# Running two first-stage units of an FFT back to back on TensorE, correction term first

## The chip, the core and the metric

The kernel runs on one core of a Trainium2 chip. The metric is the device time of one execution in microseconds (us); smaller is better. A core has a matrix engine (PE, whose weight loads the profile lists apart as PEld), a vector engine (DVE), a scalar engine (ACT), a general engine (POOL) and SP, which in this kernel only issues DMAs. Each engine takes its instructions in the order in which they stand in its own queue, and waits on semaphores for the others.

## The reference

Eight sequences of 2496 tokens with 256 channels go through a filter in the frequency domain and then through a soft mixture of experts (8 experts, 32 slots in all). All is float32.

```python
X = np.fft.rfft(x, axis=1)
y = np.fft.irfft(X * (filt_r + 1j * filt_i)[None], n=x.shape[1], axis=1)
x = y.reshape(B * S, D)
logits = x @ phi
d = softmax of logits over the tokens;  slot_input = d.T @ x
slot_out[e] = relu(slot_input[e] @ w1[e]) @ w2[e]
c = softmax of logits over the slots;   out = c @ slot_out
```

## The kernel before, in words

The transform over 2496 = 39 x 64 tokens is done in two stages of matrix products. A batch is one sequence.

**First stage** (`split_x`, `s1_unit`). The 64 columns of a batch are taken six at a time, in 11 units u per batch, b being the batch. The transform matrix and the data are each split into a high part that TensorE's float32r form holds exactly and a low part, the remainder: `w1h`, `w1l` for the matrix, `xh`, `xl` for the data. `xh` is a cast on ACT (L317), `xl` a subtraction on POOL that needs the cast (L318). The unit is then three products into one PSUM tile (L328): `w1h` with `xh`, `w1l` with `xh`, and `w1h` with `xl`, which is ready last. ACT copies the tile to `at` (L329), and SP issues a DMA of that to DRAM (`a_dram`, L333 to L336). `xh` and `xl` have three buffers each, the PSUM pool `ps_s1` two banks, `at` five buffers. One input tile `xt` (three buffers) holds the data of two units, an even one and the odd one behind it. Batch 0 takes another way into stage two (L285, L299), without the split.

**Second stage** (`x_unit`, `t_unit`). Ten steps c per batch. `ash` is read back from `a_dram` by a DMA (L349). `x_unit` multiplies it by a 128x128 matrix (L359; four matmuls in the program, eight in the trace), DVE multiplies the result by the filter's two parts (L372, L373), and the two halves are added, one on DVE (L375), one on POOL (L376, the tile `yt`). From batch 6 on, POOL does both. `t_unit` transposes `yt` on TensorE (L384), ACT copies it out to `y` (L386); at the end of a batch 40 small products make its logits (L399, `l`, 80 in the trace).

**The chain.** After every second batch a chain of further products (`chain`, L424 on) forms the maximum, the exponentials `d` and the slot sums from the two batches: `ltr`, `v`, `lg`, `mt`, `mb`, `u`, `dd`, `s`. Its steps are dealt out two at a time between the slots described next. Those of the last pair of batches run after the loop, and then come the experts and the output.

**What sets the order.** A loop over slots n, ten to a batch, puts in program order: the loads of `ash` five slots ahead, the split (`split_next`) of the units of slot n+1, then `x_unit` of n, the first-stage units whose slot is n, `t_unit` of n-2, and two steps of the chain. The slot of unit u of batch b (L679) is ten slots per batch plus min(u, 9), less five; so from batch 2 on one unit comes in each slot and units 9 and 10 share one. Batch 1's eleven units share the first five slots. After the split of an odd unit the next `xt` load is issued. A list scheduler then makes each engine's queue out of that program order, by priorities of its own; so the order on an engine has to be read from the built program. In names like `s_3_5` of that order, 3 is the batch and 5 the unit; `t_6` of the same place is `t_unit` of step 6; the last number of a name is a serial number.

Of the kernel before, what the change touches and what calls it, by code (L numbers as in the profile page):

```python
# [9 lines left out]
F32 = mybir.dt.float32  # L10
# [7 lines left out]
BATCH, SEQ, DIM = 8, 2496, 256  # L18
# [3 lines left out]
NH = 11  # L22
# [3 lines left out]
QP = PK * QR  # L26
# [24 lines left out]
AHEAD = 5  # L51
# [7 lines left out]
X0S = 4  # L59
# [149 lines left out]
def fft_soft_moe(ctx, tc, x, fr, fi, phi, w1, w2, cst, w1q, out):  # L209
    nc = tc.nc  # L210
    pe, dve, act, pool_e, sp = nc.tensor, nc.vector, nc.scalar, nc.gpsimd, nc.sync
# [3 lines left out]
    ps_s1 = ctx.enter_context(tc.tile_pool(name="ps_s1", bufs=2, space=PSUM))  # L215
# [6 lines left out]
    w1h = const.tile([KR, QP], F32R, name="w1h")  # L222
    w1l = const.tile([KR, QP], F32R, name="w1l")
# [20 lines left out]
    def open_pool(name, bufs, side):  # L244
        cm = tc.tile_pool(name=name, bufs=bufs, side=side, reuse_waits="tile")
        return cm, cm.__enter__()
# [62 lines left out]
    xhl = {}  # L309
# [8 lines left out]
        pool_e.tensor_tensor(out=xl, in0=xs, in1=xh.bitcast(F32), op=ALU.subtract)  # L318
        xhl[b, u] = xh, xl

    def s1_unit(b, u):
        if u == 0:
            a_dram[b] = scr.tile([N2, QR, DIM], F32, tag="a_dram", name=f"a_dram{b}")
        xh, xl = xhl.pop((b, u))
        ps = ps_s1.tile([QP, 2, DIM], F32, tag="s1", name=f"s1_{b}_{u}")
        at = proda.tile([QP, 2, DIM], F32, tag="at", name=f"at{b}_{u}", bufs=AB)
        for n, (w, xx) in enumerate(((w1h, xh), (w1l, xh), (w1h, xl))):
            pe.matmul(ps, w, xx, start=(n == 0), stop=(n == 2))  # L328
        act.copy(at, ps)  # L329
        k0 = PK * 2 * u  # L330
        dma = sp.dma_start
        if u < NH - 1:
            dma(a_dram[b][k0 : k0 + 2 * PK].rearrange("(i j) q d -> (j q) i d", j=PK), at)  # L333
        else:
            dma(a_dram[b][k0 : k0 + PK].rearrange("j q d -> (j q) d"), at[:, 0, :])
            dma(a_dram[b][k0 + PK], at[0:QR, 1, :])  # L336
# [6 lines left out]
    def load_ash(b, c):  # L343
        if b == 0:
            turn_ash(c)
            return
        t0 = 2 * c
        ash = prod.tile([P, 2, DIM], F32, tag="ash", name=f"ash{b}_{c}", bufs=ASH)
        sp.dma_start(ash, a_dram[b].rearrange("k (r t) d -> (k r) t d", t=NT)[:, t0 : t0 + 2, :])  # L349
        ashs[b, c] = ash  # L350

    def x_unit(b, c):

        t0 = 2 * c
        ash = ashs.pop((b, c))
        ps = ps_x.tile([P, 4, 2, 64], F32, tag="x", name=f"x_{b}_{c}")
        for k in range(2):
            for dh in range(2):
                pe.matmul(  # L359
                    ps[:, 2 * k + dh].rearrange("q r c -> q (r c)"),  # L360
                    ash[:, k, dh * P : (dh + 1) * P],
                    C("b"),
                    start=True,
                    stop=True,
                )
        frv = fr_t[:, t0 : t0 + 2].rearrange("q p h (o c) -> q (p h) o c", o=1).broadcast_to([P, 4, 2, 64])
        fiv = fi_t[:, t0 : t0 + 2].rearrange("q p h (o c) -> q (p h) o c", o=1).broadcast_to([P, 4, 2, 64])
        t2 = prod.tile([P, 4, 2, 64], F32, tag="t2", name=f"t2_{b}_{c}")
        if c % 2 == 0:
            yts[b, c // 2] = prod.tile([P, 2, 4, 2, 64], F32, tag="yt", name=f"yt_{b}_{c}", bufs=YT)  # L370
        yt = yts[b, c // 2][:, c % 2]
        dve.tensor_tensor(out=yt, in0=ps, in1=frv, op=ALU.mult)  # L372
        dve.tensor_tensor(out=t2, in0=ps[:, :, ::-1, :], in1=fiv, op=ALU.mult)  # L373
        add = pool_e if b >= PA else dve
        add.tensor_tensor(out=yt[:, :, 1, :], in0=yt[:, :, 1, :], in1=t2[:, :, 1, :], op=ALU.add)  # L375
        pool_e.tensor_tensor(out=yt[:, :, 0, :], in0=yt[:, :, 0, :], in1=t2[:, :, 0, :], op=ALU.subtract)  # L376
# [284 lines left out]
    def load_tables(c):  # L661
        lo, hi = 2 * c, 2 * c + 2
        sp.dma_start(fr_t[:, lo:hi], fr.rearrange("q (t h c) -> q t h c", h=2, c=64)[:, lo:hi])
        sp.dma_start(fi_t[:, lo:hi], fi.rearrange("q (t h c) -> q t h c", h=2, c=64)[:, lo:hi])
        for t in range(lo, hi):
            for c0, c1 in flip_runs(t) if t else ():
                sl = fi_t[:, t, :, c0:c1]
                if c <= XB:
                    dve.tensor_scalar(out=sl, in0=sl, scalar1=-1.0, scalar2=None, op0=ALU.mult)
                else:  # L670
                    act.activation(sl, sl, AF.Copy, scale=-1.0)

    CPB = NT // 2
    NS = BATCH * CPB
    units = [(b, u) for b in range(1, BATCH) for u in range(NH)]
    at_slot = {}
    for b, u in units:
        n = X0S * u // (NH - 1) if b == 1 else (b - 1) * CPB + min(u, CPB - 1) - AHEAD
        at_slot.setdefault(n, []).append((b, u))  # L679

    xnext = [(b, c) for b in range(1, BATCH) for c in range(6)]
# [5 lines left out]
    def split_next(n):  # L687
        for b, u in at_slot.get(n, ()):
            split_x(b, u)
            if u % 2 == 1 or u == NH - 1:  # L690
                next_x()
# [66 lines left out]
    def end_unit(m):  # L758
        b, c = divmod(m, CPB)
        t_unit(b, c)  # L760
        if c == CPB - 1 and b in last:
            active.append((last[b], chain(last[b])))

    last_s1 = max(at_slot)
    for n in range(NS + LT):
        if n < NS:
            if n + ASH < NS:
                load_ash(*divmod(n + ASH, CPB))
            if late:
                load_tables(late.pop(0))  # L770
            if n == CPB:
                sp.dma_start(cst_t[:, 2 * P :], cst[:, 2 * P : early])
            if n == ASH:
                x0_cm.__exit__(None, None, None)
                work_cm, work = open_pool("work", 1, "left")
            split_next(n + 1)
            if n in EARLY_L:
                for m in range(n - LT, n):
                    end_unit(m)
            with tc.issue_after(last_l[0]) if n in EARLY_L else nullcontext():  # L780
                x_unit(*divmod(n, CPB))
        for b, u in at_slot.get(n, ()):
            s1_unit(b, u)
        if n == last_s1:
            proda_cm.__exit__(None, None, None)
            late_cm, lp = open_pool("late", WL, "right")
            late_pool.append(lp)
            wl = iter(range(WL))
        if n > last_s1 and next(wl, None) is not None:
            load_ws(late_pool[0], "w", 1)  # L790
        if n >= LT and n // CPB * CPB not in [e for e in EARLY_L if e <= n < e + LT]:
            end_unit(n - LT)
        hop_slot(n)
# [100 lines left out]
    for gr in range(2):  # L894
        hsb = late_pool[0].tile([P, 2, 512], F32, tag=("ca", "hsb")[gr], name=f"hsb{gr}", bufs=1)
        for fh in range(2):
            pool, tag = ((ps_x, "x"), (ps_s1, "s1"))[gr]
# [9 lines left out]
    for gr in range(2):  # L907
        ht = late_pool[0].tile([P, 8, P], F32, tag=("cb", "cc")[gr], name=f"ht{gr}", bufs=1)
        for q in range(2):
            pool, tag = ((ps_t, "t"), (ps_c, "c"))[gr]  # L910
# [8 lines left out]
    for gr in range(2):  # L919
        pw = ps_x.tile([P, DIM], F32, tag="x", name=f"o_{gr}")  # L920
        for fc in range(8):
            for j in range(4):
                with tc.issue_after(ht_ins.ins):
# [4 lines left out]
                        start=(fc == 0),  # L928
                        stop=(fc == 7),
# [51 lines left out]
    for pos in range(BATCH):  # L981
        off = SQ * pos % P
        for m in range((off + SQ) // P):
            cols.append((sts[pos], m * P))
            g, n = nout[0], len(cols)
# [47 lines left out]
```

## Time and profile before

| what | value |
|---|---|
| time, median of 3 runs | 366.56 us (365.73 to 367.51) |
| the profiled execution | 366.22 us |
| its span, first to last instruction | 364.4 us |
| mean granted clock of TensorE | 0.972 |
| DMA traffic | 103.59 MB, mean 284 GB/s |
| matmul instructions | 4111 |

The profile is of one execution, 366.22 us long by its own time, of which the span from the first to the last instruction is 364.4 us. A row of its table of groups has the line and engine, the operation, the tiles written and read, their shapes and how many there were, then the total busy time and the mean duration in ns, and the idle time of that engine just before such instructions with what ended it. In the chain of waits each row is a piece of the path that ended last: start, length, engine, line and how many instructions. In the timeline a row has start, length, what ran and how many, and in brackets the idle time before it. Matmuls overlap in the array, so the length of a matmul is more than what it adds to a run of them; the distance from start to start tells that. In the table by stretches the columns are the stretch, its length, then busy time and count for PE, PEld, DVE, ACT and POOL, the granted clock, and the busy share of the DMA engines with what they moved.

### The profile page before, as it was taken

How to read it: one execution, taken by the hardware profiler on the slowest of the kernel's cores; microseconds unless marked ns; L12 is line 12 of the kernel's file. 1: busy time of each engine (PE TensorE's matmuls, PEld its weight loads, DVE VectorE, ACT ScalarE, POOL GpSimd, SP SyncE). 2: the span in 40 equal slices, each digit the busy share in tenths (PEclk: the TensorE clock that was granted, in tenths of full speed). 3: DMA queues.
4: the chain of work that ended last, by engine and by line, in shares of the span. 5: the costliest groups of instructions: out<-in, count | busy, mean ns of one | idle time of the engine just before them, and what ended most of it. 6: DMA issues, size and time to landing. Idle time of an engine off the chain costs nothing.

```text
span 364.4 us, 10525 instructions
## 1 busy us (share of the span) xinstructions
PE 341.4 (94%) x4111; PEld 284.0 (78%) x4111; DVE 267.0 (73%) x457; ACT 212.3 (58%) x433; POOL 198.4 (54%) x229
## 2 busy tenths in 40 slices
PE   8999999989999999999999999999999999999950
PEld 8899688779888868988887889898766546888840
DVE  2799839948879986969898865999545733777650
ACT  3788768666786758478766654444533321665540
POOL 0389988986774856668578474665800112252200
PEclk9999999999999999999999999999999999998695
DMA  7999999897797777949967873733699995899996
GB/s 252 378 296 329 303 359 388 256 350 284 204 335 273 214 258 231 351 135 314 333 161 221 257 224 103 236 84 91 215 379 385 360 373 184 335 416 411 413 417 263
DMA packets 53668, 103.59 MB, mean 284 GB/s; under 512 B 5407, under 2 KB 26143, under 8 KB 51315
## 3 DMA queue, kind: packets, MB, share of 16 engines
q1 hardware_dynamic: 53619, 102.92, 81.8%
q8 instruction: 33, 0.54, 0.6%
q14 instruction: 16, 0.13, 0.1%
HBM read 62.78 MB, written 40.12 MB: 282 GB/s over the span
## 4 chain that ended last, share of the span: by engine, by line
PE 77%; DVE 6%; DMA 5%; POOL 3%; issue 2%; ACT 2%; SPq 1%; DVEq 0%; POOLq 0%; ACTq 0%
PE x L359 18%; PE s L328 14%; PE t L384 8%; PE out L968 7%; PE s L619 5%; PE l L399 3%; DMA xt<-in_x 3%; PE lg L500 3%; PE v L470 2%; PE u L553 2%; PE o L924 2%; PE h L901 2%; PE dd L578 2%; DMA last_lg<-in_w 2%; POOL yt L376 1%
## 5 line engine op out<-in xcount | busy, mean ns | idle before, releaser
L318 POOL TENSOR_TENSOR xl<-xt,xh 117x512 fp32r<-117x512 f32 x77 | 100.6, 1315 | 42.5 <-ACT xh L317 34.0
L359 PE MATMUL x<-cst_t,ash 128*128 128x128 f32 x640 | 87.5, 277 | 1.2 <-PE s L328 0.8
L359 PEld LDWEIGHTS x<-cst_t,ash 128*128 128x128 f32 x640 | 80.9, 191 | 8.1 <-issue 2.1
L376 POOL TENSOR_TENSOR yt<-yt,t 128x256 f32<-128x256 f32 x80 | 66.1, 829 | 21.9 <-DVE t L373 18.1
L372 DVE TENSOR_TENSOR yt<-x,fr_t 128x512 f32<-128x512 f32 x80 | 54.6, 682 | 28.4 <-PE x L359 17.7
L317 ACT CAST xh<-xt 117x512 fp32r<-117x512 f32 x77 | 47.7, 622 | 27.4 <-PE s L328 10.1
L386 ACT COPY y<-t 128x512 f32<-128x512 f32 x80 | 47.2, 591 | 19.2 <-PE t L384 18.7
L373 DVE TENSOR_TENSOR t<-x,fi_t 128x512 f32<-128x512 f32 x80 | 54.3, 678 | 0.0
L384 PE MATMUL t<-cst_t,yt 128*128 128x128 f32 x320 | 50.2, 274 | 2.1 <-POOL yt L376 2.1
L375 DVE TENSOR_TENSOR yt<-yt,t 128x256 f32<-128x256 f32 x60 | 48.6, 819 | 1.1
L329 ACT COPY at<-s 120x512 f32<-120x512 f32 x77 | 44.9, 584 | 5.1 <-PE s L328 4.3
L384 PEld LDWEIGHTS t<-cst_t,yt 128*128 128x128 f32 x320 | 38.4, 141 | 11.7 <-issue 4.1
L328 PE MATMUL s<-xh,w1h 117*120 117x512 f32 x77 | 37.0, 480 | 0.0
L328 PE MATMUL s<-xl,w1h 117*120 117x512 f32 x77 | 31.9, 415 | 0.5 <-POOL xl L318 0.3
L328 PE MATMUL s<-xh,w1l 117*120 117x512 f32 x77 | 30.4, 395 | 0.0
L968 PE MATMUL out<-so_h,st 32*128 32x256 f32 x312 | 29.7, 331 | 0.7 <-DVE ob L977 0.2
L968 PE MATMUL out<-so_l,st 32*128 32x256 f32 x312 | 28.7, 310 | 0.5 <-issue 0.5
L977 ACT COPY ob<-out 128x512 f32<-128x512 f32 (+1 forms) x42 | 21.7, 560 | 10.5 <-PE out L968 8.4
L977 DVE COPY ob<-out 128x512 f32<-128x512 f32 (+1 forms) x42 | 24.9, 646 | 3.4 <-PE out L968 3.2
L968 PEld LDWEIGHTS out<-so_h,st 32*128 32x128 f32 x312 | 22.6, 206 | 3.4 <-DVE ob L977 0.8
L375 POOL TENSOR_TENSOR yt<-yt,t 128x256 f32<-128x256 f32 x20 | 15.6, 779 | 17.1 <-DVE t L373 12.0
L968 PEld LDWEIGHTS out<-so_l,st 32*128 32x128 f32 x312 | 23.5, 207 | 0.9 <-issue 0.6
(124 smaller groups left out, 502.3 us busy)
## 6 DMA issues: line engine op xcount, KB each, us to landing
out<-ob SPq DMA_DIRECT2D x18, 1024.0 KB
xt<-in_x SPq DMA_DIRECT2D x35, 512.0 KB
ash<-a_dram SPq DMA_DIRECT2D x70, 256.0 KB
a_dram<-at SPq DMA_DIRECT2D x70, 240.0 KB
w<-in_w SPq DMA_DIRECT2D x62, 256.0 KB
xt<-in_x SPq DMA_DIRECT2D x18, 256.0 KB
c_dram<-lg SPq DMA_DIRECT2D x2, 643.5 KB
cl<-c_dram SPq DMA_DIRECT2D x2, 643.5 KB
```

The source lines that it names most:

```text
L317: act.copy(xh, xs)
L318: pool_e.tensor_tensor(out=xl, in0=xs, in1=xh.bitcast(F32), op=ALU.subtract)
L328: pe.matmul(ps, w, xx, start=(n == 0), stop=(n == 2))
L359: pe.matmul(ps[:, 2 * k + dh].rearrange("q r c -> q (r c)"), ash[:, k, dh * P : (dh + 1) * P], C("b"), start=True, stop=True,)
L372: dve.tensor_tensor(out=yt, in0=ps, in1=frv, op=ALU.mult)
L373: dve.tensor_tensor(out=t2, in0=ps[:, :, ::-1, :], in1=fiv, op=ALU.mult)
L375: add.tensor_tensor(out=yt[:, :, 1, :], in0=yt[:, :, 1, :], in1=t2[:, :, 1, :], op=ALU.add)
L376: pool_e.tensor_tensor(out=yt[:, :, 0, :], in0=yt[:, :, 0, :], in1=t2[:, :, 0, :], op=ALU.subtract)
L384: pe.transpose(pt[:, k, dh, :], yt[:, c % 2, 2 * k + dh].rearrange("q r c -> q (r c)"), ident)
L386: act.copy(y, pt.rearrange("k p h d -> k p (h d)"))
L968: last_mm[0] = nc.tensor.matmul(prs[k][:, mm, :], st[q, n % 2, c0 : c0 + P], (so_h, so_l)[n // 2][q, :], start=(n == 0), stop=(n == 3),).ins
L977: copied[k % 2] = copy(ob[:, nm * k : nm * (k + 1), :], prs[k]).ins
```

## The change

`s1_unit` becomes `s1_units`, which takes a list of units of one batch. It makes the PSUM tiles of all of them, then issues the products from the last unit back to the first, each unit's three in the order (`w1h`, `xl`), (`w1l`, `xh`), (`w1h`, `xh`). Every product but the first stands in a context (`glued`) that puts it behind the first on TensorE and gives it a high priority in the scheduler. The copies to `at` and the DMAs follow, in the units' order. In batches 2 to 7 the loop gives it an even unit and the odd one behind it together, and to that end the odd unit is moved into the even one's slot, one slot earlier, with its split. Unit 10 is alone, and so are all units of batch 1; these have the new order of their three products, but no partner. The arithmetic is the same.

```diff
+    def s1_units(b, us):
+        if us[0] == 0:
             a_dram[b] = scr.tile([N2, QR, DIM], F32, tag="a_dram", name=f"a_dram{b}")
+        ts = {}
+        for u in us:
+            ts[u] = ps_s1.tile([QP, 2, DIM], F32, tag="s1", name=f"s1_{b}_{u}")
+        first = None
+        for u in reversed(us):
+            xh, xl = xhl.pop((b, u))
+            for n, (w, xx) in enumerate(((w1h, xl), (w1l, xh), (w1h, xh))):
+                with glued(first):
+                    ins = pe.matmul(ts[u], w, xx, start=(n == 0), stop=(n == 2)).ins
+                first = first or ins
+        for u in us:
+            s1_out(b, u, ts[u])
...
-        for n, (w, xx) in enumerate(((w1h, xh), (w1l, xh), (w1h, xl))):
-            pe.matmul(ps, w, xx, start=(n == 0), stop=(n == 2))
...
-        n = X0S * u // (NH - 1) if b == 1 else (b - 1) * CPB + min(u, CPB - 1) - AHEAD
+        n = X0S * u // (NH - 1) if b == 1 else (b - 1) * CPB + min(u // 2 * 2, CPB - 1) - AHEAD
...
-        for b, u in at_slot.get(n, ()):
-            s1_unit(b, u)
+        todo = list(at_slot.get(n, ()))
+        while todo:
+            b, u = todo.pop(0)
+            us = [u]
+            if b >= 2 and u % 2 == 0 and (b, u + 1) in todo:
+                todo.remove((b, u + 1))
+                us.append(u + 1)
+            s1_units(b, us)
```

The lines below the edit have moved by 17 to 24: L359 is L376 in the changed kernel, L376 is L393, L384 is L401, L399 is L416. Three places show what the scheduler makes of it. First TensorE in the second half of batch 3's first stage, while batch 1 is in the second stage. Before:

```order
L384 MATMUL t_6_1055<-cst_t,yt_6_980 128x128 x4
L328 MATMUL s_3_4_1080<-xh_4_1033,w1h 120x512
L328 MATMUL s_3_4_1080<-xh_4_1033,w1l 120x512
L328 MATMUL s_3_4_1080<-xl_4_1034,w1h 120x512
L384 MATMUL t_7_1087<-cst_t,yt_6_980 128x128 x4
L328 MATMUL s_3_5_1111<-xh_5_1064,w1h 120x512
L328 MATMUL s_3_5_1111<-xh_5_1064,w1l 120x512
L328 MATMUL s_3_5_1111<-xl_5_1065,w1h 120x512
L384 MATMUL t_8_1118<-cst_t,yt_8_1043 128x128 x4
```

The same engine and place in the changed kernel:

```order
L401 MATMUL t_6_1061<-cst_t,yt_6_993 128x128 x4
L401 MATMUL t_7_1094<-cst_t,yt_6_993 128x128 x4
L339 MATMUL s_3_5_1081<-xl_5_1045,w1h 120x512
L339 MATMUL s_3_5_1081<-xh_5_1044,w1l 120x512
L339 MATMUL s_3_5_1081<-xh_5_1044,w1h 120x512
L339 MATMUL s_3_4_1080<-xl_4_1041,w1h 120x512
L339 MATMUL s_3_4_1080<-xh_4_1040,w1l 120x512
L339 MATMUL s_3_4_1080<-xh_4_1040,w1h 120x512
L401 MATMUL t_8_1124<-cst_t,yt_8_1056 128x128 x4
L401 MATMUL t_9_1157<-cst_t,yt_8_1056 128x128 x4
```

Units 4 and 5 stand together and start with `xl` of unit 5; the transposes stand in twos around them. In 28 of the 30 pairs the six products are one run, in most of them with the two units' products mixed; in the pairs 0, 1 and 2, 3 of batch 3 an `x_unit` stands between the units. Second, POOL a little earlier in the same batch, before:

```order
L318 TENSOR_TENSOR xl_1_938<-xt_0_808,xh_1_937 117x512
L318 TENSOR_TENSOR xl_2_971<-xt_1_864,xh_2_970 117x512
L376 TENSOR_TENSOR yt_4_908<-yt_4_908,t_1_4_907 128x4x64
L376 TENSOR_TENSOR yt_4_908<-yt_4_908,t_1_5_948 128x4x64
L318 TENSOR_TENSOR xl_3_1002<-xt_1_864,xh_3_1001 117x512
L318 TENSOR_TENSOR xl_4_1034<-xt_2_870,xh_4_1033 117x512
L376 TENSOR_TENSOR yt_6_980<-yt_6_980,t_1_6_979 128x4x64
L376 TENSOR_TENSOR yt_6_980<-yt_6_980,t_1_7_1012 128x4x64
```

The same engine and place in the changed kernel:

```order
L318 TENSOR_TENSOR xl_0_906<-xt_0_736,xh_0_905 117x512
L318 TENSOR_TENSOR xl_1_910<-xt_0_736,xh_1_909 117x512
L393 TENSOR_TENSOR yt_4_921<-yt_4_921,t_1_4_920 128x4x64
L393 TENSOR_TENSOR yt_4_921<-yt_4_921,t_1_5_948 128x4x64
L318 TENSOR_TENSOR xl_2_978<-xt_1_844,xh_2_977 117x512
L318 TENSOR_TENSOR xl_3_982<-xt_1_844,xh_3_981 117x512
L393 TENSOR_TENSOR yt_6_993<-yt_6_993,t_1_6_992 128x4x64
L393 TENSOR_TENSOR yt_6_993<-yt_6_993,t_1_7_1012 128x4x64
```

The two subtractions in a row are now those of one pair, where before they were the odd unit of one and the even unit of the next. Third, TensorE around `u`, the products behind the exponentials of the first chain, before (the first row is `mb`, whose result the exponentials wait for):

```order
L523 MATMUL mb_1447<-dg,ones 128x32
L399 MATMUL l_0_1768<-yt_0_1106,phi_t 32x128 x8
L399 MATMUL l_0_1768<-yt_2_1233,phi_t 32x128 x8
L399 MATMUL l_0_1768<-yt_4_1358,phi_t 32x128 x8
L399 MATMUL l_0_1768<-yt_6_1466,phi_t 32x128 x8
L399 MATMUL l_4_1801<-yt_8_1599,phi_t 32x128 x7
L553 MATMUL u_0_1487<-cst_t,d_1450 64x60 x16
```

The same engine in the changed kernel, from the last of the logits of the same batch on (`mb` stands four rows ahead of the first row shown, with 21 logit products between):

```order
L416 MATMUL l_4_1808<-yt_8_1612,phi_t 32x128 x8
L376 MATMUL x_2_1849<-cst_t,ash_2_1533 128x128 x4
L339 MATMUL s_4_9_1888<-xl_9_1844,w1h 120x512
L339 MATMUL s_4_9_1888<-xh_9_1843,w1l 120x512
L339 MATMUL s_4_8_1887<-xl_8_1840,w1h 120x512
L339 MATMUL s_4_9_1888<-xh_9_1843,w1h 120x512
L339 MATMUL s_4_8_1887<-xh_8_1839,w1l 120x512
L339 MATMUL s_4_8_1887<-xh_8_1839,w1h 120x512
L376 MATMUL x_3_1877<-cst_t,ash_3_1594 128x128 x4
L401 MATMUL t_0_1860<-cst_t,yt_0_1709 128x128 x4
L401 MATMUL t_1_1901<-cst_t,yt_0_1709 128x128 x4
L570 MATMUL u_0_1493<-cst_t,d_1457 64x60 x16
```

A pair, two `x_unit`s and two transposes have come in front of `u`. From step 6 of batch 6's second stage on, TensorE's order is the same in both kernels.

More of the change, by code (lines that the diff above doesn't have):

```diff
@@ L319, in split_x, with glued, s1_out @@
         xhl[b, u] = xh, xl
-    def s1_unit(b, u):
-        if u == 0:
-            a_dram[b] = scr.tile([N2, QR, DIM], F32, tag="a_dram", name=f"a_dram{b}")
-        xh, xl = xhl.pop((b, u))
-        ps = ps_s1.tile([QP, 2, DIM], F32, tag="s1", name=f"s1_{b}_{u}")
+    def glued(first):
+        cm = ExitStack()
+        if first is not None:
+            cm.enter_context(tc.issue_after(first))
+            cm.enter_context(tc.high_priority())
+        return cm
+    def s1_units(b, us):
+        if us[0] == 0:
+            a_dram[b] = scr.tile([N2, QR, DIM], F32, tag="a_dram", name=f"a_dram{b}")
+        ts = {}
[10 more added lines that the diff above has]
+            s1_out(b, u, ts[u])
+    def s1_out(b, u, ps):
         at = proda.tile([QP, 2, DIM], F32, tag="at", name=f"at{b}_{u}", bufs=AB)
-        for n, (w, xx) in enumerate(((w1h, xh), (w1l, xh), (w1h, xl))):
-            pe.matmul(ps, w, xx, start=(n == 0), stop=(n == 2))
         act.copy(at, ps)
```

## Prediction

> **What bounds the kernel now.** I read the page first, then the busy times by stretch, then the chain of waits, and last the timelines of single engines. The page's head and the groups that the change touches:
>
> ```profile
> span 364.4 us, 10525 instructions
> L318 POOL TENSOR_TENSOR xl<-xt,xh 117x512 fp32r<-117x512 f32 x77 | 100.6, 1315 | 42.5 <-ACT xh L317 34.0
> L376 POOL TENSOR_TENSOR yt<-yt,t 128x256 f32<-128x256 f32 x80 | 66.1, 829 | 21.9 <-DVE t L373 18.1
> L317 ACT CAST xh<-xt 117x512 fp32r<-117x512 f32 x77 | 47.7, 622 | 27.4 <-PE s L328 10.1
> L328 PE MATMUL s<-xh,w1h 117*120 117x512 f32 x77 | 37.0, 480 | 0.0
> L328 PE MATMUL s<-xl,w1h 117*120 117x512 f32 x77 | 31.9, 415 | 0.5 <-POOL xl L318 0.3
> L328 PE MATMUL s<-xh,w1l 117*120 117x512 f32 x77 | 30.4, 395 | 0.0
> ```
>
> TensorE sits idle for half a microsecond in front of these products, all told; so the wait for `xl` that the new order is about is small already. By stretch (the columns begin with PE, PEld, DVE, ACT, POOL):
>
> ```profile
> 15.00:40.81 25.81, 25.37 (x187) 22.84 (x186) 25.07 (x42) 22.37 (x58) 23.20 (x21) 1.00 0.98 328
> 40.81:78.44 37.63, 34.19 (x291) 27.81 (x294) 26.21 (x36) 25.82 (x50) 34.12 (x32) 1.00 0.95 327
> 78.44:225.10 146.66, 146.39 (x1781) 125.52 (x1781) 122.68 (x200) 97.82 (x190) 98.70 (x97) 1.00 0.78 249
> ```
>
> From 78 to 225 us, where the last first-stage product ends, PE is full: 146.39 of 146.66. From 40.8 to 78.4 PE and POOL are both short of full, by about 3.5 us each, with the DMA engines at 0.95. There the chain of waits leaves PE:
>
> ```profile
> 40.81 0.72 PE s L328 x3
> 41.56 1.55 POOL xl L318 x2
> 43.71 0.92 POOL yt L376
> 45.82 0.74 POOL yt L376
> 50.04 1.09 PE x L359 x8
> 52.95 0.55 PE ltr L457 x5
> 56.69 0.44 PE t L384 x4
> 69.89 0.86 POOL yt L376
> 70.75 2.69 POOL xl L318 x2
> 73.44 0.69 POOL yt L376
> 75.96 1.79 PE x L359 x16
> 77.75 0.69 PE s L328 x3
> 78.44 2.32 PE l L399 x80
> ```
>
> How much PE really stands idle there follows from its work. Between 40.81 and 78.44 it does 18 units at 0.69, twelve `x_unit`s at 0.89 (half of 1.79), thirteen `t_unit`s at 0.44, the logits at 2.32 with the 0.2 that the `x_unit` behind them takes longer, and `ltr` at 0.55: 12.4 + 10.7 + 5.7 + 2.5 + 0.6 = 31.9 of 37.6 us. So **5.7 us are idle in that stage**, and hardly any in the next 147.
>
> **What an unbroken run saves on PE.** The first product of a unit lasts 480 ns by the page and the second 395, which looks like 85 ns for each entry. Starts tell otherwise:
>
> ```profile
> 55.74 0.48 PE L328 MATMUL s<-xh,w1h 117*120 117x512 f32 x1
> 56.06 0.40 PE L328 MATMUL s<-xh,w1l 117*120 117x512 f32 x1
> 56.30 0.39 PE L328 MATMUL s<-xl,w1h 117*120 117x512 f32 x1
> 56.53 0.60 PE L384 MATMUL t<-cst_t,yt 128*128 128x128 f32 x4
> ```
>
> Products are 0.23 to 0.24 apart, the first and second 0.32; but the unit as a whole takes 0.69 to 0.70 in the chain, which is three times 0.23. The first product starts early, in the shadow of its neighbour, by what it then lasts longer. So 32 entries fewer (some 81 runs before, 49 now) save at most 0.01 each: 0.3, taken as nothing. The products are as many as before, and the weights are loaded as often. The Trainium skill, page "TensorE: Matmul & The Clock Gate", section "LDWEIGHTS (loading the stationary operand)", gives a load as columns over 1.2 in ns: 100 ns for these 120 columns. If each entry exposed one such load, 32 fewer would save 3.2 us by that figure; the starts above don't show it.
>
> **The stage from 41 to 78 us, walked through.** I walk the changed order from the end of `xl` of batch 2's unit 1 (P), after which its first pair can start. Prices: `xl` 1.29, POOL's `yt` 0.91, pair 1.39. And a loop: the end of a pair frees the `xh` buffer of the unit three ahead, ACT casts, POOL subtracts, and only then the next pair's first product may start.
>
> ```profile
> 36.70 1.55 POOL L318 TENSOR_TENSOR xl<-xt,xh 117x512 fp32r<-117x512 f32 x1 [0.66 <-ACT xh L317]
> 38.91 1.46 POOL L318 TENSOR_TENSOR xl<-xt,xh 117x512 fp32r<-117x512 f32 x1
> 55.62 1.28 POOL L318 TENSOR_TENSOR xl<-xt,xh 117x512 fp32r<-117x512 f32 x1
> 56.54 0.62 ACT L317 CAST xh<-xt 117x512 fp32r<-117x512 f32 x1 [0.83 <-PE s L328]
> ```
>
> The cast started 0.08 after the product at 56.06 had ended. So the loop is 0.1 + 0.62 + 0.05 + 1.29 + 0.1 = 2.2 us. Before, P is 40.4 (38.91 + 1.46). The changed order puts one `yt` more ahead of it on POOL; in the 0.66 idle ahead of 36.70 this fits or not: P is 40.4 to 41.1.
>
> Then, after P: pair 0, 1 until 1.5; step 9's `yt` ends at 3.1 (`yt`, `xl`, `yt` on POOL), where PE waits 1.2; `xl` of unit 3 ends at 4.4, where it waits 0.9; logits to 8.1; pair 4, 5 to 9.6; two `x_unit`s and `ltr` to 12.3, where pair 6, 7 is ready (its loop ended at 11.7). With two `x_unit`s and two `t_unit`s between pairs, 2.66 us, the loop is covered, and PE goes on unbroken to batch 3's unit 1 at 22.0. From there POOL's two `xl` and two `yt` (4.4 us) and PE's work per two slots (4.05) are nearly even; PE waits 0.3 for unit 3. Ahead of pair 4, 5 there stand only two transposes (0.88) behind unit 2, so it waits 1.2, and ahead of 6, 7 0.3. The pair 6, 7 ends and the logits of batch 1 start at P + 36.6. These waits come to 3.9, against 5.7 before. The logits then start at 77.0 to 77.7 instead of 78.44; I take the middle, **1.1 us earlier**, with P's two ends as bounds and as much again either way for landings of `xt`, with the DMA engines at 0.95.
>
> One rule speaks against this. The Trainium skill, page "SBUF — State Buffer", section "SBUF: two separate sides", says that DVE with two SBUF inputs and GpSimd share a port pair as an exclusive lock, whose loser blocks for the whole instruction. The adds show such a thing:
>
> ```profile
> 53.57 1.50 DVE L375 TENSOR_TENSOR yt<-yt,t 128x256 f32<-128x256 f32 x1
> 65.50 0.42 DVE L375 TENSOR_TENSOR yt<-yt,t 128x256 f32<-128x256 f32 x1
> ```
>
> The same add takes 0.42 or 1.50. If ten adds of this stage came behind an `xl` for 0.6 us longer than now, DVE would lose 6 us; but pairs of `xl` stood back to back before too (70.75), and each `x_unit` has DVE work for only 1.36 + add, in slots of 2.2 or more. I take nothing.
>
> **The start.** In batch 1, `xl` now heads each unit. Before, two products of unit 0 ran while PE waited for the last data of batch 0:
>
> ```profile
> 15.18 0.49 PE L328 MATMUL s<-xh,w1h 117*120 117x512 f32 x1
> 15.51 0.40 PE L328 MATMUL s<-xh,w1l 117*120 117x512 f32 x1
> 16.31 1.10 PE L299 MATMUL ash<-cst_t,spec 128*128 128x128 f32 x8 [0.40 <-ACT spec L292]
> ```
>
> These 0.46 us now come after 16.31, in a stretch where PE has no slack. Nothing if POOL and the landings set P anyway, 1.0 if other heads wait too; I take 0.2, near the lower end, since the row at 36.70 shows P set from ACT and a load.
>
> **From 78 to 225 us.** Pairs stand 2.8 to 3.5 us of PE work apart (two `x_unit`s and two `t_unit`s, 2.66, and chain products), one pair of each chain 2.2: the loop of 2.2 fits. What can go is the wait at `u`:
>
> ```profile
> 108.69 0.30 PE L523 MATMUL mb<-dg,ones 128*128 128x32 f32 x2
> 111.23 2.43 PE L553 MATMUL u<-cst_t,d 117*64 117x60 f32 x64
> 177.68 2.43 PE L553 MATMUL u<-cst_t,d 117*64 117x60 f32 x64
> 242.26 2.08 PE L553 MATMUL u<-cst_t,d 117*64 117x60 f32 x64
> ```
>
> Covered `u` takes 2.08, in the first two chains 2.43. The work between `mb` and `u` grows from 2.4 us (the logits) to 1.7 + 1.8 + 1.4 + 0.9 = 5.8, so the wait goes: 2 x 0.35 = **0.7 us**. It could be zero if the exponentials on DVE and ACT now stand later in their queues. Copies and DMAs: two `at` come together, 1.2 us of ACT, ahead of which the next cast stands in most places; no load of `ash` follows sooner than before, since unit 10 still ends a batch. Behind 225 us nothing moves.
>
> **Sum.** 366.2 - 1.1 + 0.2 - 0.7 = **364.6 us** (the profiled execution of 366.22 is 0.3 under the median). Terms at their bounds give 363.0 to 366.2.
>
> **Rivals.**
> - *Entries do cost what the page's durations say* (85 ns). 32 x 0.085 = 2.7 on top: 361.9 us. Against it stands the 0.70 per unit. The Trainium skill's rule on loads, cited above, would be its mechanism.
> - *All the waits of the stage go*, since a run that has begun never stops: 366.2 - 5.7 - 0.7 = 359.8. Against it: 0.88 us between two pairs doesn't cover a loop of 2.2.
> - *Slower: the loop is longer than the PE work between pairs*, and the head of a run, waiting for `xl`, holds up all of PE behind it. At 3.5 us (one more POOL `yt`, 0.91, and a stretched `xl`, in the loop) the gaps of batches 4 to 7 that are shorter (2.8 to 3.3; five, twice over) fall short by 2.1 us per two batches, 4.2 in all, and the early stage loses its gain: 366.2 + 4.2 - 0.7 = 369.7. It decides where the loop passes 2.8. For it: POOL's `xl` waited 34.0 us for casts before, the start included. Against: PE was full while it did.
> - *No change: loads, not the order, set the early stage*, with `u` as it was: 366.2. For it: DMA engines at 0.95 to 0.98 until 78 us. Against: the chain there names POOL and PE.
>
> **How the numbers follow.** Forecast 0.46, entries 0.13, all waits 0.07, slower 0.19, no change 0.15. A measurement of this kernel tells about 0.5%, 1.8 us, from no change, so "faster" begins at 364.4. Of the forecast's 0.46 a bit under half, 0.22, lies below that. Faster 0.13 + 0.07 + 0.22 = 0.42; same 0.24 + 0.15 = 0.39; slower 0.19. The range reaches from the entries' case to 368.2, into the slower one; left out are the 0.07 and about 0.1 of the slower. The forecast's own range is 363.0 to 366.2.
>
> **What would show it.** In the changed profile the logits of batch 1 start near 77.3; the group of heads (`s` from `xl`) has idle time in front of it, ahead of batch 2's pair 2, 3 and batch 3's pair 4, 5; a pair lasts 1.39 from its first start to the next instruction's; `u` takes 2.1 in all chains; PE has no gap over 0.3 at heads after 78. I am wrong if pairs take 1.3 or less, if heads wait in every batch, or if the part behind 225 gets longer or shorter.

## The result, and the profile after

The changed kernel takes 369.22 us (median of 8 runs, 367.98 to 372.27), the kernel before 366.86 us beside it: a ratio of 1.0083 (95% interval 1.0055 to 1.0111), so 3.0 us slower by the ratio, where 1.6 us faster was forecast. Here and below a ratio compares the fast executions alone, so it need not equal that of the medians, which are 2.4 us apart here. The profiled execution took 367.98 us, the fastest of the eight, so its trace shows only a part of the loss. The page's head and the groups that were shown of before:

```profile
span 365.9 us, 10467 instructions
L318 POOL TENSOR_TENSOR xl<-xt,xh 117x512 fp32r<-117x512 f32 x77 | 100.0, 1306 | 41.7 <-ACT xh L317 41.6
L393 POOL TENSOR_TENSOR yt<-yt,t 128x256 f32<-128x256 f32 x80 | 66.9, 841 | 19.4 <-DVE t L390 18.7 <-PE v L487 0.5
L317 ACT CAST xh<-xt 117x512 fp32r<-117x512 f32 x77 | 47.9, 625 | 28.1 <-PE s L339 19.2 <-DMA xt<-in_x 4.2 <-POOL xl L318 2.6
L339 PE MATMUL s<-xl,w1h 117*120 117x512 f32 x77 | 35.0, 455 | 1.8 <-POOL xl L318 0.8 <-ACT xh L317 0.8
```

Casts now wait 19.2 us for the end of first-stage products (10.1 before), and POOL waits 41.6 us for casts (34.0 before). The heads on PE wait 1.8 us in all. Ahead of batch 2's pair 2, 3 and batch 3's pair 4, 5 they wait as forecast, though less than the 0.9 and 1.2 of the walk:

```profile
46.04 0.50 PE L339 MATMUL s<-xl,w1h 117*120 117x512 f32 x1 [0.57 <-POOL xl L318]
73.23 0.49 PE L339 MATMUL s<-xl,w1h 117*120 117x512 f32 x1 [0.78 <-ACT xh L317]
```

By stretch, the same three as before:

```profile
15.00:40.81 25.81, 23.97 (x176) 21.51 (x177) 24.74 (x41) 21.41 (x55) 22.38 (x21) 1.00 0.94 302
40.81:78.44 37.63, 34.94 (x295) 29.55 (x294) 24.08 (x37) 26.69 (x52) 34.05 (x31) 1.00 0.96 328
78.44:225.10 146.66, 146.46 (x1771) 124.93 (x1770) 116.81 (x197) 95.96 (x192) 99.41 (x97) 1.00 0.79 254
```

PE has lost 1.4 us up to 40.8 us (23.97 against 25.37), and is full behind 78 us as before. Where the loss begins, PE's timeline shows:

```profile
14.25 0.72 PE L285 MATMUL s<-w1q_t,xt 117*128 117x120 f32 x5
16.48 1.09 PE L299 MATMUL ash<-cst_t,spec 128*128 128x128 f32 x8 [1.50 <-ACT spec L292]
```

The two products that filled this gap before 16.31 are gone from it: 1.50 us idle instead of 0.40. POOL's timeline has the end of P, `xl` of batch 2's unit 1, and the chain of waits goes from there to the logits of batch 1:

```profile
40.47 1.28 POOL L318 TENSOR_TENSOR xl<-xt,xh 117x512 fp32r<-117x512 f32 x1
```

```profile
47.35 6.35 DMA xt<-in_x
53.73 0.63 ACT xh L317
54.43 1.30 POOL xl L318
...
71.61 1.07 ACT at L346 x2
72.68 0.53 ACT xh L317
...
77.84 1.40 PE s L339 x6
79.24 2.32 PE l L416 x80
```

P is 41.75, where 40.4 to 41.1 was forecast; the logits start at 79.24 instead of 77.0 to 77.7. On the way there is a load of `xt` of 6.35 us, and a cast that stands behind two copies to `at`. A pair takes 1.40, as forecast (1.39). The covered `u`:

```profile
116.83 2.08 PE L570 MATMUL u<-cst_t,d 117*64 117x60 f32 x64
184.13 2.08 PE L570 MATMUL u<-cst_t,d 117*64 117x60 f32 x64
243.78 2.08 PE L570 MATMUL u<-cst_t,d 117*64 117x60 f32 x64
```

Its wait is gone from both chains, as forecast.

### The profile page after: what moved, and what is told of

Read it like the earlier page. It is cut to its first block, busy times and chain, and to the rows that moved or that the text cites. A ratio compares the mean times of both kernels' runs of the same rounds, so it can differ in the third digit from the quotient of the medians.

```text
span 365.9 us, 10467 instructions
## 1 busy us (share of the span) xinstructions
PE 339.0 (93%) x4111; PEld 281.9 (77%) x4111; DVE 260.0 (71%) x457; ACT 210.7 (58%) x433; POOL 198.4 (54%) x229
## 4 chain that ended last, share of the span: by engine, by line
PE 57%; DVE 15%; DMA 10%; POOL 7%; issue 4%; ACT 2%; SPq 1%; DVEq 0%; POOLq 0%
PE x L376 12%; PE s L339 10%; PE out L991 5%; PE t L401 5%; POOL xl L318 5%; DMA xt<-in_x 5%; PE s L636 4%; DVE t L390 3%; DVE yt L389 3%; PE l L416 3%; DMA out<-ob 3%; POOL yt L393 3%; PE u L570 2%; PE v L487 2%; PE lg L517 2%
## 5 line engine op out<-in xcount | busy, mean ns | idle before, releaser
L318 POOL TENSOR_TENSOR xl<-xt,xh 117x512 fp32r<-117x512 f32 x77 | 100.0, 1306 | 41.7 <-ACT xh L317 41.6
L376 PE MATMUL x<-cst_t,ash 128*128 128x128 f32 x640 | 87.3, 277 | 0.1
L376 PEld LDWEIGHTS x<-cst_t,ash 128*128 128x128 f32 x640 | 80.0, 191 | 4.3 <-issue 1.2
L393 POOL TENSOR_TENSOR yt<-yt,t 128x256 f32<-128x256 f32 x80 | 66.9, 841 | 19.4 <-DVE t L390 18.7
L317 ACT CAST xh<-xt 117x512 fp32r<-117x512 f32 x77 | 47.9, 625 | 28.1 <-PE s L339 19.2
L401 PE MATMUL t<-cst_t,yt 128*128 128x128 f32 x320 | 48.2, 273 | 1.2 <-POOL yt L393 1.2
L401 PEld LDWEIGHTS t<-cst_t,yt 128*128 128x128 f32 x320 | 38.2, 141 | 11.1 <-issue 5.6
L346 ACT COPY at<-s 120x512 f32<-120x512 f32 x77 | 42.0, 586 | 6.8 <-PE s L339 6.5
L392 DVE TENSOR_TENSOR yt<-yt,t 128x256 f32<-128x256 f32 x60 | 44.8, 759 | 0.8
L339 PE MATMUL s<-xl,w1h 117*120 117x512 f32 x77 | 35.0, 455 | 1.8 <-POOL xl L318 0.8
L339 PE MATMUL s<-xh,w1h 117*120 117x512 f32 x77 | 30.3, 393 | 0.0
L991 PE MATMUL out<-so_h,st 32*128 32x256 f32 x312 | 27.4, 308 | 0.7 <-DVE ob L1000 0.2
L991 PE MATMUL out<-so_l,st 32*128 32x256 f32 x312 | 25.9, 285 | 0.0
L991 PEld LDWEIGHTS out<-so_h,st 32*128 32x128 f32 x312 | 20.4, 183 | 3.6 <-DVE ob L1000 1.3
L416 PE MATMUL l<-yt,phi_t 128*32 128x128 f32 x640 | 21.1, 275 | 0.2
```

What stands on the lines that cost most here:

```text
L317: act.copy(xh, xs)
L339: ins = pe.matmul(ts[u], w, xx, start=(n == 0), stop=(n == 2)).ins
L376: pe.matmul(ps[:, 2 * k + dh].rearrange("q r c -> q (r c)"), ash[:, k, dh * P : (dh + 1) * P], C("b"), start=True, stop=True,)
L401: pe.transpose(pt[:, k, dh, :], yt[:, c % 2, 2 * k + dh].rearrange("q r c -> q (r c)"), ident)
L991: last_mm[0] = nc.tensor.matmul(prs[k][:, mm, :], st[q, n % 2, c0 : c0 + P], (so_h, so_l)[n // 2][q, :], start=(n == 0), stop=(n == 3),).ins
```

## The experiments

The change has four parts: the new order of the products in batch 1; that order from batch 2 on, with its glue; the odd unit's earlier slot; and the pair, six products in one run. Each ratio is to the kernel before on the same chip, with its 95% interval. The runs come from three chips, so two ratios that are compared can be of different chips. Diffs are against the changed kernel unless they say otherwise.

### Batch 1 and the rest

Batch 1 back as it was:

```diff
-            for n, (w, xx) in enumerate(((w1h, xl), (w1l, xh), (w1h, xh))):
-                with glued(first):
+            for n, (w, xx) in enumerate(
+                ((w1h, xh), (w1l, xh), (w1h, xl)) if b == 1 else ((w1h, xl), (w1l, xh), (w1h, xh))
+            ):
+                with glued(first if b > 1 else None):
```

> The changed kernel with batch 1's units in the order that they had before (the two products of xh first, xl last, nothing glued); pairs and the xl-first order from batch 2 on stay. Theory A (the start): the new order of batch 1 holds the xh buffers longer and leaves PE idle at 15 us, and that delays batch 2's unit 1 by 1.5 us, which is kept to the end. Then this kernel takes 366.5 to 367.5, 2 us less than the changed one, its 13th xl starts at 38.9 us, not 40.5, and the logits of batch 1 start at 77 to 78. Theory B (the pairs: a longer loop and waits in the batches from 2 on): 369 as the changed one, with the 13th xl at 38.9 and the delay arising behind it. Theory C (the xl-first order itself, in any batch): 368.

368.58 us, ratio 1.0067 (1.0040 to 1.0095). Theory A falls as the whole cause: most of the loss stays. The 13th `xl` starts at 39.4 us, and the logits of batch 1 begin at 77.9 as A had it, but the last of them starts only at 81.9, with a pair in their middle. The converse of this kernel has the new order in batch 1 alone (the two orders exchanged in the lines above, and no pairs, no move):

```diff
-        n = X0S * u // (NH - 1) if b == 1 else (b - 1) * CPB + min(u // 2 * 2, CPB - 1) - AHEAD
+        n = X0S * u // (NH - 1) if b == 1 else (b - 1) * CPB + min(u, CPB - 1) - AHEAD
...
-            if b >= 2 and u % 2 == 0 and (b, u + 1) in todo:
+            if False:
```

> The kernel before with the new order of products and the glue in batch 1 alone; no pairs, no unit moved, old order from batch 2 on. Theory A (the start): 368.4 to 369.2, slower than before by 1.5 to 2.3 us, with 1.5 us of PE idle at 15 us and the 13th xl at 40.5. Theory B (the pairs): 366.9, the start's delay being taken up by the idle time of 41 to 78 us. Theory C (the xl-first order in any batch): 367.3, as one batch of seven.

367.06 us, ratio 1.0038 (1.0014 to 1.0061): 1.4 us slower, just under what theory A gave. Its timeline of PE has the gap again, a little wider:

```profile
13.80 1.73 PE L285 MATMUL s<-w1q_t,xt 117*128 117x120 f32 x14
17.24 0.98 PE L299 MATMUL ash<-cst_t,spec 128*128 128x128 f32 x7 [1.71 <-ACT spec L292]
```

So batch 1's order costs something by itself, and is not the main part of the change's loss.

### The order alone, and the pairs without it

Batch 1 as before, the new order and the glue from batch 2 on, but single units in their old slots (the two edits above together, except the exchange):

> From batch 2 on the new order of the three products and the glue, but single units in their old slots; batch 1 as before. Theory A (the start): 366.5 to 367.2, as before. Theory B (the pairs): 366.9. Theory C (a head that waits for xl holds up PE for longer, in any batch): 368.5 or more, with idle time before the heads of over 3 us.

364.22 us, ratio 0.9952 (0.9924 to 0.9981). No theory had this: the order by itself makes the kernel *faster*. Then the pairs with the old order in them:

```diff
-            for n, (w, xx) in enumerate(((w1h, xl), (w1l, xh), (w1h, xh))):
-                with glued(first):
+            for n, (w, xx) in enumerate(((w1h, xh), (w1l, xh), (w1h, xl))):
+                with glued(first if b > 1 else None):
```

> Pairs from batch 2 on, in one glued run of six, but each unit's products in the order of before (xl last); batch 1 as before. Theory A (the start): within 0.7 of the kernel with batch 1 as before, so 366.3 to 367.7. Theory B (the pairs): 369 as the changed kernel. Theory C (xl first costs): 1 us or more below the kernel with batch 1 as before.

371.48 us, ratio 1.0147 (1.0107 to 1.0187), slower than any theory said. So theory C is wrong in sign (in single units xl first with its glue is worth 0.5% against the kernel before; in glued pairs the order by itself is worth 0.8%), and B is right that the pairs, with the slot that comes with them, cost.

### The slot and the run of six

The odd unit's slot moved, nothing else (no pairs, old order, no glue):

```diff
-            for n, (w, xx) in enumerate(((w1h, xl), (w1l, xh), (w1h, xh))):
-                with glued(first):
+            for n, (w, xx) in enumerate(((w1h, xh), (w1l, xh), (w1h, xl))):
+                with glued(None):
...
-            if b >= 2 and u % 2 == 0 and (b, u + 1) in todo:
+            if False:
```

> The kernel before with the odd unit moved into the even one's slot from batch 2 on, and nothing else: single units, old order of products, batch 1 as before. Theory L (the loop: with three buffers of xh and xl, a run of six holds two of them to its end, so that the next cast, subtraction and head start later): as the kernel before within 0.5%, since single units free their buffers one by one. Theory S (the moved slot itself, by which two units come together and two slots later none): 2 us or more slower than before, as the pairs are. Theory X (the load of xt starts later, and the cast waits for it): between the two, with more than 8 us of casts waiting for xt.

368.54 us, ratio 1.0065 (1.0039 to 1.0092). The move costs 2.4 us without a single pair. This is theory S; casts waited for `xt` for 6.9 us, not over 8, so X has nothing from this run. With xl first and glue as well:

> Single units with xl first, each glued in itself, the odd unit moved into the even one's slot, batch 1 as before. Measured so far against the kernel before: xl first alone 0.9952, the moved slot alone 1.0065, both with the pair 1.0067. Theory S (the moved slot costs, the run of six nothing): 1.0067, as with the pair. Theory R (the run of six costs, too): xl first and the slot add up, 1.0017, and the pair itself costs the other 0.5%.

367.14 us, ratio 1.0022 (0.9995 to 1.0048): what theory R had, the two effects added up. The run of six then accounts for the step from 1.0022 to 1.0067, though the intervals overlap. Pairs in the odd unit's slot instead:

```diff
+... min(u // 2 * 2 + 1, CPB - 1) - AHEAD
```

> Pairs with xl first and batch 1 as before, but the even unit is moved into the odd one's slot, one slot later, instead of the odd one one slot earlier. Theory X (loads of xt): the loads have one slot more, and the time falls by 1.5 us or more against the pairs in the even slot, to 367 or less. Theory L (the loop): 368 to 369, as the loop and the distance from pair to pair are the same. Theory D (the second stage is fed too late): slower than 369, since unit 8 and 9 of a batch and unit 10 come together at its end.

370.58 us, ratio 1.0122 (1.0080 to 1.0165): slower still, as theory D said, and against X. In its profile nothing is lost up to 92 us (it is 0.2 us ahead of before there, by the measure used further down), and the expert products, behind the last chain, start 2.8 us later than before. That fits D, whose reason was not tested by itself.

### Buffers

These keep batch 1 as before, pairs and xl first. Four buffers of `xh` and `xl`, paid for with two of `at`:

```diff
-AB = 5
+AB = 3
...
-        xh = proda.tile([KR, 2, DIM], F32R, tag="xh", name=f"xh{b}_{u}", bufs=3)
-        xl = proda.tile([KR, 2, DIM], F32R, tag="xl", name=f"xl{b}_{u}", bufs=3)
+        xh = proda.tile([KR, 2, DIM], F32R, tag="xh", name=f"xh{b}_{u}", bufs=4)
+        xl = proda.tile([KR, 2, DIM], F32R, tag="xl", name=f"xl{b}_{u}", bufs=4)
```

> Pairs with xl first and batch 1 as before, but four buffers of xh and of xl; the room comes from at, which has three instead of five. Theory L (the loop): the casts no longer wait for the end of a run; 2 us or more less than the same kernel with three buffers, so 366.5 or less. Theory X (loads of xt): 368 to 369 as with three buffers, with the casts waiting for the DMA as long as there. Three buffers of at may cost something under either theory, which would show as waits of the copies for the DMA.

373.73 us, ratio 1.0231 (1.0180 to 1.0283). Four of `xt` (`bufs=XB + 1`), with three of `at` again:

> Pairs with xl first and batch 1 as before, but four buffers of xt (the room again from at, three instead of five). Theory X (loads of xt): the casts wait less for the DMA (under 4 us instead of 10), and the time is 367 or less. Theory L (the loop): 368 to 369, with the casts waiting for PE as long as before.

370.14 us, ratio 1.0119 (1.0078 to 1.0160). Neither can be read by itself, since no run has three buffers of `at` and nothing else. In the first, ACT's waits between 14 and 110 us (total, times, longest) read:

```profile
ACT at L348 <- DMA a_dram<-at: 10.4, 8, 3.1
...
ACT xh L317 <- PE s L341: 2.7, 3, 1.5
```

The copies wait 10.4 us for the DMA that empties `at` (10.9 in the second kernel; in the pairs with five buffers there is no such wait). A fourth `xh` alone costs only one buffer of `at`, and has a control with three:

> Pairs with xl first and batch 1 as before, with four buffers of xh and still three of xl; at has four instead of five. Theory L (the loop over the end of a run to the next cast): the casts wait for PE under 4 us between 14 and 110 us (9.4 with three buffers), and the time is 1.5 us or more below the same kernel with three buffers of xh and four of at. Rival: the casts wait for something else instead (loads of xt, POOL), and the time stays.

> The control for the four xh buffers: pairs with xl first, batch 1 as before, three buffers of xh, four of at. If the copies to at have room, 368.6 as with five; if at is short, slower, with copies that wait for the DMA (with three buffers of at they waited 10 to 11 us between 14 and 110 us, and that may be all that the two kernels with three lost).

369.20 us, ratio 1.0084 (1.0055 to 1.0114), and for the control 368.62 us, 1.0073 (1.0044 to 1.0101). The control equals five buffers of `at`, so this comparison is clean. ACT's waits, first of the control, then with four `xh`:

```profile
ACT xh L317 <- PE s L341: 9.3, 7, 2.9
ACT xh L317 <- DMA xt<-in_x: 6.7, 7, 2.5
```

```profile
ACT xh L317 <- DMA xt<-in_x: 10.5, 10, 2.3
ACT xh L317 <- PE s L341: 5.8, 6, 1.5
```

The casts wait 3.5 us less for PE and 3.8 us more for the loads, and the time stays, as the rival had it. Theory L is not refuted by that: `xl` still has three buffers, and POOL's subtractions, which never waited for PE in the control, now do:

```profile
POOL xl L318 <- PE s L341: 5.7, 5, 2.7
```

So the loop over the end of a run was not opened; it now closes over the buffers of `xl`. How firmly the loads took the place of PE these rows cannot say, since waits for loads differ by as much between two profiles of one kernel (3.1 and 7.1 us, below). The Trainium skill, page "Perfetto Trace Analysis", section "Optimization Strategy", says that consistent bubbles can mean too little room for the next tile. A buffer more for the tile with the wait did not help here (1.0084 against 1.0073); part of the wait went to the next tile, `xl`.

### Order and glue apart

In single units, old slots, batch 1 as before: first xl first without the glue (`glued(None)`), then the glue with xl last.

> Single units with xl first from batch 2 on, in their old slots, but not glued: the scheduler may put other work between a unit's products. Batch 1 as before. If the order of the products is what helps, 364.2 as with the glue (ratio 0.995); if it is the glue, that keeps other work out of a unit, 366 as before.

> Single units in their old slots, xl last as before, glued from batch 2 on: only the scheduler's freedom to part a unit's products is taken away. With the order but no glue it was 0.9996, with both 0.9952. If the glue alone does it: 0.995, 364.4. If it takes both (a glued unit whose last product waits for xl holds PE in its middle): slower than before, 1.002 to 1.006.

366.10 us, ratio 0.9996 (0.9971 to 1.0022), and 368.16 us, ratio 1.0050 (1.0029 to 1.0071). It takes both: without the glue the new order brings nothing that can be measured, and a glued unit that ends with the operand made last costs 1.8 us.

### Which batches pay, and batch 1 without pairs

The same kernels with pairs from batch 4 on, and with pairs in batches 2 and 3 alone (the conditions `b >= 2` and the slot's `u // 2 * 2` limited to these batches), the other units single and glued:

> Single glued units with xl first in batches 2 and 3, pairs in the even unit's slot from batch 4 on; batch 1 as before. Theory E (the pairs cost only in the early stage, up to 82 us, where POOL, the loads and PE are all nearly full): 364.0 to 365.0, a ratio of 0.995 as with single units throughout. Theory G (a pair costs in any batch): four of six batches paired, so 0.67 of the way from 0.995 to 1.007: 1.003, or 367.

> The converse: pairs in the even unit's slot in batches 2 and 3 alone, single glued units with xl first from batch 4 on; batch 1 as before. Theory E (the early stage): 1.006 to 1.007, 368.5, as with pairs throughout. Theory G (any batch): a third of the way, 0.999, 365.8.

366.36 us, ratio 1.0015 (0.9985 to 1.0045), and 368.67 us, ratio 1.0068 (1.0043 to 1.0094). Pairs in two batches cost as much as pairs in six; this is theory E. But pairs from batch 4 on cost as well, 0.6% against single units, which is theory G. The two don't add up, and neither theory is whole. Last, single glued units in all batches, batch 1 among them:

> Single glued units with xl first in all batches, batch 1 too, in their old slots. Batch 1's new order cost 0.38% when the rest was as before and 0.16% beside the pairs. If it delays the start for good: 0.9952 + 0.0038 = 0.999, 365.8. If the stage behind it takes up the delay where it has room: 0.9952 to 0.997, 364.5 to 365.1.

366.61 us, ratio 0.9999 (0.9978 to 1.0021): batch 1's order takes back all that the single units gain, some 0.5%, so without pairs its delay is lasting.

### How much one profile can say

The kernel with pairs from batch 4 on has, on every engine, the same instructions in the same order as that with single units until past 85 us. Yet their logits of batch 1 lie (first and last start):

```profile
L418 PE MATMUL l<-yt,phi_t x80: 272/273/297, 78.5 to 80.6; 128*32 128x128 f32 x80
```

```profile
L418 PE MATMUL l<-yt,phi_t x80: 272/273/297, 75.5 to 77.6; 128*32 128x128 f32 x80
```

The second, single units, is 3.0 us earlier. So I profiled the single units and the pairs (batch 1 as before) once more:

> The kernel with single glued units and xl first from batch 2 on, a second time on another day of the chip. Up to the end of batch 3's units its instructions stand in the same order on PE as in the kernel with pairs from batch 4 on, yet in the two profiled runs the logits of batch 1 begin some 3 us apart. If the early stage is a matter of the order, this run's logits of batch 1 begin near 75.5 us again, and the ratio is 0.993 to 0.998. If it varies from run to run, they begin anywhere from 75.5 to 79, and the profile of one run cannot say where a kernel loses 2 us.

> The kernel with pairs and batch 1 as before, a second time beside it: the ratio 1.004 to 1.0095 again, the logits of batch 1 beginning at 78 us and ending at 82. If the early stage is set by the order, the distance of 3 to 4 us from the single units at the end of those logits returns; if it varies from run to run, it may not, while the medians still differ by 1.1%.

363.97 us, ratio 0.9919 (0.9898 to 0.9940), and 368.73 us, ratio 1.0051 (1.0029 to 1.0072). The medians repeat, and the single units are the best version, faster than both kernels. Their profile doesn't repeat in the early stage:

```profile
L418 PE MATMUL l<-yt,phi_t x80: 272/273/297, 77.4 to 79.5; 128*32 128x128 f32 x80
```

That is 1.9 us later than in the first one, with the same program, and the casts waited for loads for 7.1 us there up to 110 us, against 3.1. The two profiled executions themselves took 365.86 and 363.89 us, so they differ in time by about what the profiles differ in this stage. They are also from two chips, so chip and execution are not told apart; but on the chip of the first alone the executions of this kernel reach from 362.05 to 365.82 us. To separate the stages, I gave each matmul the median distance to the next start that its kind (the tile that it writes, and the shapes) has in before's trace, added these up along each trace, and read the clock where the sum is 80 and 210 us (92 and 243 us in before). Ahead (-) or behind before, in us:

| kernel | at 80 | at 210 | between |
|---|---|---|---|
| changed | +0.8 | +1.5 | +0.7 |
| pairs, batch 1 as before, first profile | +1.5 | +2.2 | +0.7 |
| the same, second profile | +0.5 | +1.2 | +0.7 |
| single units, batch 1 as before, first profile | -2.2 | -3.1 | -1.0 |
| the same, second profile | -0.3 | -1.3 | -1.0 |

Up to 92 us two profiles of one kernel differ by 1.0 and 1.8 us; behind it they agree within 0.1. There PE never waits visibly, and what differs is which products stand next to each other. Rows of PE's timeline, first of the changed kernel, then of the single units:

```profile
109.59 0.86 PE L416 MATMUL l<-yt,phi_t 128*32 128x128 f32 x22
110.38 0.41 PE L540 MATMUL mb<-dg,ones 128*128 128x32 f32 x2
110.72 1.93 PE L416 MATMUL l<-yt,phi_t 128*32 128x128 f32 x58
112.58 0.60 PE L376 MATMUL x<-cst_t,ash 128*128 128x128 f32 x3
```

```profile
106.54 0.30 PE L542 MATMUL mb<-dg,ones 128*128 128x32 f32 x2
106.77 2.38 PE L418 MATMUL l<-yt,phi_t 128*32 128x128 f32 x78
109.09 0.33 PE L572 MATMUL u<-cst_t,d 117*64 117x60 f32 x4
```

The same `mb` and 80 logits take 2.99 us from start to start (112.58 - 109.59) where `mb` cuts the logits, and 2.55 for 78 of them where it does not, which makes about 2.6 for 80: a cut costs some 0.4 us.

## Why the prediction was wrong

**The stage from 41 to 78 us, and the pairs: the step that failed.** The walk gave the rest of the change, without batch 1, 1.8 us of gain (1.1 there, 0.7 at `u`); measured it is 0.5 to 0.7% of loss, 1.9 to 2.5 us. The traces show the walk's own step. It has the logits of batch 1 start at P + 36.6, so the last of the 80, 2.1 us behind the first in before, at P + 38.7. Measured from P to the start of the last one:

| kernel | P | from P to the last logit |
|---|---|---|
| before | 40.4 | 40.1 |
| changed | 41.75 | 39.5 |
| pairs, batch 1 as before, two profiles | 40.7, 39.7 | 41.2, 41.2 |
| pairs in batches 2 and 3 alone | 40.3 | 40.7 |
| single units, batch 1 as before, two profiles | 41.0, 41.1 | 36.7, 38.4 |

In single units some 0.7 us more of PE's work stands behind the last logit; in the others the work ahead of it is the same. So the walk gave the pairs 1.4 us of gain in this stage, and with batch 1 as before they lost 0.6 to 1.1 us in it, in three profiles. In the changed kernel the stage gains 0.6, but behind a P that is 1.4 us later.

The walk had one loop, and took each cast to start 0.1 us after a run's end with its `xt` there. I priced the moved slot at nothing beyond its place in the walk. It costs 0.65% alone, and the run of six adds 0.3 to 0.5% (1.0051 and 1.0067 against 1.0022 with xl first; with xl last the step from 1.0065 to 1.0147 also holds the glue, which cost 0.5% there in single units). The order with its glue gives 0.5 to 0.8%. The change carries a gain and two losses that together are larger, and I had put the gain down to all three.

Which wait makes the losses is not shown. ACT's waits between 14 and 110 us, before, then the changed kernel, then pairs with batch 1 as before, then single units:

```profile
ACT xh L317 <- DMA xt<-in_x: 7.6, 9, 1.8
...
ACT xh L317 <- PE s L328: 4.3, 7, 0.9
ACT at L329 <- PE s L328: 2.9, 4, 1.5
```

```profile
ACT xh L317 <- PE s L339: 7.2, 11, 1.5
ACT xh L317 <- DMA xt<-in_x: 4.2, 5, 1.9
ACT at L346 <- PE s L339: 4.0, 6, 1.2
```

```profile
ACT xh L317 <- DMA xt<-in_x: 10.2, 8, 2.9
ACT xh L317 <- PE s L341: 9.4, 10, 2.4
...
ACT at L348 <- PE s L341: 1.1, 3, 0.5
```

```profile
ACT at L348 <- PE s L341: 12.9, 21, 1.4
ACT xh L317 <- DMA xt<-in_x: 3.1, 4, 1.2
...
ACT xh L317 <- PE s L341: 0.7, 2, 0.4
```

In this run of the pairs the casts waited 19.6 us for the two together, against 11.9 before and 3.8 in single units. (The second profiles have 19.3 and 7.5.) But these totals do not measure the loss. In the changed kernel the casts waited 11.4 us, no more than before, and in single units ACT's copies to `at` waited 12.9 us for PE instead. That two units now come together and then none, and wait in turn for buffers, loads and copies, is argued, not shown: which of these waits sets the cost of the slot and of the six stays open, and more buffers of several kinds at once, without fewer of `at`, were not tried.

**The sum's bounds** were added up too narrowly on the slow side: logits 0.4 us later, 1.0 at the start and nothing at `u` make 367.6, not 366.2. The measured time lies above that as well.

**The start**: priced at 0.2 with an upper end of 1.0. Alone it costs 1.4 us (0.38%), beside single glued units some 0.5%, beside the pairs 0.16 to 0.3%, which the intervals can't tell from nothing. The gap is where I saw it. The reason for the lower end, that POOL and the landings set P anyway, did not hold: POOL works without a break from 27.6 us to P in the changed kernel, but that work had itself slipped, and P came 1.4 us later. With batch 1's order alone P is 42.5. With batch 1 as before it is 39.7 to 41.1 in the profiles of the table, but 42.7 in that of the pairs from batch 4 on; so it is the medians (0.38%), not P in single profiles, that show what batch 1's order costs.

**Behind 78 us**: the wait at `u` went (2.08 three times), worth 0.7. It went in single units, too, where the distance from `mb` to `u` is 2.55 us as before (2.54), so more work between the two was not needed for it. And the stretch between 92 and 243 us as a whole lost 0.7, so that 1.4 us were lost elsewhere in it. This is the second step that failed: I wrote that only `u` can move there. By the measure of the table of distances, the chain's other products (`ltr`, `v`, `lg`, `mb`, `dd`) took 1.2 us more than before, and the first stage, `x` and `t` together 0.2 more. The cuts in the chain's own products had moved, which the order of the changed program showed.

**Entries**: right. A pair takes 1.40, and the chain of waits before has 0.69 to 0.70 for a single unit. So 32 entries fewer saved nothing like 2.7 us. The Trainium skill's rule on loads (page "TensorE: Matmul & The Clock Gate", section "LDWEIGHTS (loading the stationary operand)") gives 100 ns for such a load; the trace of before lists these loads at 181 to 185 ns each, and no entry here exposed one.

**The slower rival** had the time (369.7 against 369.2) by luck, not the mechanism. It wanted gaps at heads in batches 4 to 7; heads wait 1.8 us in the whole profile, PE is full behind 78 us, and pairs in batches 2 and 3 alone cost as much as all.

**DVE** did not lose the time that pairs of `xl` might have cost it: its busy time fell, from 267.0 to 260.0 us in all, and in each of the three stretches (24.08 against 26.21 us in the middle one). The lock of which the Trainium skill speaks (page "SBUF — State Buffer", section "SBUF: two separate sides") cost nothing more here than before.

**Behind 225 us** nothing moved, as forecast: the start of the expert products shifted by 1.5 us (290.3 to 291.8), the delay that the table has at 210.

## What to carry to other kernels

Take a change apart before pricing it: here the order of three products with its glue is worth 0.5 to 0.8%, and the moved slot and the pairing that came with it cost more. Two units together and then none can be dearer than one at a time, although the work is the same: here the move alone cost 0.65%, and pairs cost both in the stage where several engines and the loads are nearly full and behind it. Start an unbroken run with the operand made last, but not where PE has nothing else to do until it is there, as at the start here.

## What the runs showed of the hardware

- Two profiles of the same program, single units, on two chips, had the logits of batch 1 at 75.5 and 77.4 us. The stretch ahead of them has DMA engines at 0.9 to 1.0 and waits for loads. Behind 92 us the two keep their distance within 0.1 us. A loss of 2 us in a loaded stage can't be placed from one profile; medians of 6 to 12 runs had intervals of 0.2 to 0.5% either way.
- On a full PE the neighbours count: the same products took 0.7 us more or 1.0 us less over some 150 us, to 0.1 us alike in two profiles, with no idle time that the trace lists.
